# Sums of a Strassen first product made in PSUM instead of by VectorE additions

## The chip, the cores and the metric

The kernel runs on one core of one Trainium2 chip. The metric is the device time in microseconds (us) of one execution; four runs of the kernel before lie between 708.72 and 708.87 us with a median of 708.79. A profile is one such execution, recorded by the hardware.

## The reference, cut to what matters

```python
# x: (8, 8, 512, 64)   state: (8, 8, 32, 64)
a     = softmax(x @ state^T / 8)              # over the 32 states
xread = a @ state                             # 512 tokens a batch
sread = softmax(state @ x^T / 8) @ x          # 32 tokens a batch
t = concat([xread, sread], axis=2) -> (8*544, 512)
h = t @ w_in                                  # 512 -> 2048
g = h * sigmoid(1.702 * h)
out = g @ w_out                               # 2048 -> 512
```

All of it is float32. The loop that matters here is the first product `h` for the 512 `xread` tokens of a batch. The kernel never forms `xread`: per batch it multiplies `state` into `w_in` once (the tiles `M`, 256 rows of head and state by 2048) and then makes `h` as attention weights times `M`, a product over 256 instead of 512.

## The kernel before, in words

All instructions are put in order by the program text (`manual_schedule`): each engine works through its own list in that order, and a semaphore wait that Tile adds stops everything behind it on that engine.

Batches 0 and 1 go through plain products (`up_x`, `down`, lines 524 and 542) while the weights arrive. Batches 2 to 7 and, last, the 256 `sread` tokens ("sr") use Strassen's scheme in Winograd's form, in which a product of 2 x 2 blocks takes seven block products and some sums instead of eight block products.

The first product of such a stage is `up_strassen` (line 1031). It makes `h` in four blocks u = 0..3. A block holds four rooms in SBUF, `c11`, `c12`, `c21`, `c22`: two tiles of 128 rows of `h` from the lower half of the 2048 and two from the upper half, each for the first and the second 256 tokens. Each of the seven block products is four matmul records of 128x128 by 128x256 in the trace (two matmuls, each run as two passes), all recorded at line 1051. Three PSUM banks serve a block: `x` in one of two banks of the pool `psH`, `y` and `z` in two of the four fixed banks `bank_o`. TensorE gathers in a bank only what lies in one chain of matmuls. Where the scheme adds a product to two places, VectorE does it. In the code of before, with `P1` for `l11*b11`:

- `begin(u)` makes `P1` in `x`, ScalarE copies it to `c21` (line 1074); `y = m2*t2`; VectorE writes `c12 = y + c21`.
- `middle(u)` makes `z = m1*t1`; `x += l12*b21`, and gelu of it goes to `c11`; `y += l21*t3`; VectorE writes `c22 = y + c21` and then `c22 = z + c22`; gelu in place.
- `end(u)` makes `y += l22*t4`, VectorE writes `c21 = y + c21`, gelu in place; `z += m4*b22`, VectorE writes `c12 = z + c12`, gelu in place. It is called one block later, after `begin(u + 1)`.

That is five additions of 128x512 on VectorE a block (line 1061, the helper `add`), one copy (line 1074) and four gelus (line 1058) on ScalarE. `s12` (lines 565 and 566) and `s3` (line 571) are the sums of finished rooms that the second product wants: `s12(u - 1)` stands at the end of `end(u)`, and all four `s3` in `rest`. `rest` also holds `end(3)`; it is called from a hook inside the second product's first block product, `P1` of `strassen_two` (line 738), after half of it. `between` puts two sums of the left operands on VectorE after block 0 and two after block 1. The `sr` stage has half as many tokens and no `between`, but ten VectorE steps in `beside`, of which `aside` takes one at three places in each block.

The second product, `strassen_two`, is again Winograd's scheme, five of whose block products are split once more (`strassen_low`, matmuls at line 689); the softmax of the next batch is hung into it by hooks. Its last low product ends just before `up_strassen` of the next batch; it leaves two reads of `psH` banks by VectorE (line 694) behind.

Of the kernel before, what the change touches and what calls it, by code (L numbers as in the profile page):

```python
# [10 lines left out]
FP32 = mybir.dt.float32  # L11
# [3 lines left out]
ALU = mybir.AluOpType  # L15
# [5 lines left out]
def kernel(  # L21
# [30 lines left out]
    nc = tc.nc  # L52
# [5 lines left out]
    P = 128  # L58
# [5 lines left out]
    FC = 512  # L64
# [22 lines left out]
    psH = ctx.enter_context(tc.tile_pool(name="psH", bufs=2, space=bass.MemoryType.PSUM))  # L87
# [4 lines left out]
    def att_ps(shape, name):  # L92
        return psA.tile(shape, FP32, tag="att", name=name)
# [26 lines left out]
    bank_o = [psO.tile([P, FC], FP32, tag=f"o{i}", name=f"o_{i}") for i in range(4)]  # L120
# [72 lines left out]
    for i, v in enumerate((8.0 * most, 8.0 * (most - least))):  # L193
        t = konst.tile([P, 1], FP32, name=f"edge_{i}")
# [360 lines left out]
    def quarters(key, u, ntok):  # L555

        g, half = G[key, u], ntok // 2
        return g[:, :, :half], g[:, :, half:ntok]

    def s12(key, u, ntok):  # L560

        half = ntok // 2
        (a11, a21), (_, a22) = quarters(key, u, ntok), quarters(key, HF // 2 + u, ntok)
        s1, s2 = S1[:, 2 * u : 2 * u + 2, :half], S2[:, 2 * u : 2 * u + 2, :half]
        nc.vector.tensor_tensor(out=s1, in0=a21, in1=a22, op=ALU.add)
        nc.vector.tensor_tensor(out=s2, in0=s1, in1=a11, op=ALU.subtract)

    def s3(key, u, ntok):

        a11, a21 = quarters(key, u, ntok)  # L570
        nc.vector.tensor_tensor(out=a21, in0=a11, in1=a21, op=ALU.subtract)
# [58 lines left out]
    NU, QT = HF // 2, S // 2  # L630
# [400 lines left out]
    def up_strassen(b, ntok, left, right, between=(), beside=()):  # L1031


        beside = list(beside)
        QT = ntok // 2
        b11, b21, b22, t1, t2, t3, t4 = right
        banks = {}

        def product(u, bank, lhs, rhs, first):
            if first:  # L1040
                if bank == "x":
                    banks[bank, u] = psH.tile([P, 2, QT], FP32, tag="h", name=f"upx_{b}_{u}")
                else:
                    o = bank_o[2 * (u % 2) + (bank == "z")]
                    banks[bank, u] = o[:, : 2 * QT].rearrange("p (k t) -> p k t", k=2)
            ps = banks[bank, u]
            n = len(lhs)
            for k in range(2):
                o = 2 * P * (u % 2) + P * k
                for i in range(n):  # L1050
                    nc.tensor.matmul(  # L1051
                        ps[:, k], lhs[i][:, o : o + P], rhs[i],
                        start=(first and k == 0 and i == 0), stop=(i == n - 1), skip_group_check=True,
                    )
            return ps

        def gelu(dst, src):
            nc.scalar.activation(out=dst, in_=src, func=AF.Gelu_apprx_sigmoid)  # L1058

        def add(ps, x, dst):  # L1060
            nc.vector.tensor_tensor(out=dst, in0=ps, in1=x, op=ALU.add)  # L1061

        def aside():
            if beside:
                fn, args = beside.pop(0)
                fn(*args)


        def begin(u):
            l11, l12, l21, l22, m1, m2, m4 = left(u)  # L1070
            G[b, u], G[b, NU + u] = free.pop(0), free.pop(0)
            _, c12 = quarters(b, u, ntok)
            c21, _ = quarters(b, NU + u, ntok)
            nc.scalar.copy(c21, product(u, "x", l11, b11, True))
            add(product(u, "y", m2, t2, True), c21, c12)
            aside()

        def middle(u):
            l11, l12, l21, l22, m1, m2, m4 = left(u)
            c11, c12 = quarters(b, u, ntok)  # L1080
            c21, c22 = quarters(b, NU + u, ntok)
            z = product(u, "z", m1, t1, True)
            gelu(c11, product(u, "x", l12, b21, False))
            add(product(u, "y", l21, t3, False), c21, c22)
            add(z, c22, c22)
            gelu(c22, c22)
            aside()

        def end(u):
            l11, l12, l21, l22, m1, m2, m4 = left(u)  # L1090
            c11, c12 = quarters(b, u, ntok)
            c21, c22 = quarters(b, NU + u, ntok)
            add(product(u, "y", l22, t4, False), c21, c21)
            gelu(c21, c21)
            add(product(u, "z", m4, b22, False), c12, c12)
            gelu(c12, c12)
            aside()
            if u:
                s12(b, u - 1, ntok)

        for u in range(NU):
            begin(u)
            if u:
                end(u - 1)
            middle(u)
            for fn, args in between[u] if u in between else ():
                fn(*args)

        def rest():
            end(NU - 1)  # L1110
            s12(b, NU - 1, ntok)
            for u in range(NU):
                s3(b, u, ntok)

        return rest

# [151 lines left out]
    for b in range(1, B):  # L1268
        if b > 1:
            ahead = {"P1a": [(up_strassen(b, S, *parts_x(b), A[b]["sums"]), ())]}  # L1270
        else:
            ahead = {
                "P1a": [(low_third, (B22,)), (T_of, (T4, B21, T2)), (low_third, (T2,)), (low_away, (4, T4)), (low_third, (T4,))]
            }
# [4 lines left out]
        else:  # L1279

            steps, left, right = sr_sums()
# [12 lines left out]
        k = 3 if b + 1 < B else 0  # L1294
# [6 lines left out]
    strassen(  # L1301
        "sr", B * Ns, lambda r, n: out_s[nb * r.start : nb * r.stop, :, n],
        [[(up_strassen("sr", B * Ns, left, right, beside=beside), ())]],
    )

# [29 lines left out]
```

## Time and profile before

| | |
|---|---|
| median of the runs | 708.79 us |
| the profiled execution | 708.87 us, of which the span in the trace is 707.1 us |
| a batch's stage, from one `up_strassen` to the next | 75.63 us (280.22 less 204.59) |
| of it, from the first matmul of `up_strassen` to the first at line 738 | 22.45 us |
| share of the span, PE / DVE / ACT | 98% / 85% / 33% |
| `add` at line 1061 | 140 instructions, 88.0 us |
| gelus at line 1058 | 84 from SBUF, 49.8 us; 24 + 4 from PSUM |
| copy at line 1074 | 24 of 128x512, median 0.571 us; 4 of 128x256, 0.354 us |

PE is TensorE's matmuls and PEld its loads of the stationary operand, which run beside the matmul ahead; DVE is VectorE, ACT ScalarE. A matmul's length in the trace is longer than the time to the next one, since matmuls are pipelined; here the time between starts counts.

### The profile page before, as it was taken

The page shows a single profiled execution, that of the slowest core. Times are in us where ns is not written, and L with a number is a line of the kernel's source. Part 1 is how long each engine was busy: PE and PEld are TensorE (multiplying, and loading weights), DVE is VectorE, ACT ScalarE, POOL GpSimd, SP SyncE. Part 2 cuts the span into 40 slices and gives each one's busy share as a digit, 9 for nine tenths or more (in the row PEclk, how much of TensorE's full clock was granted, in tenths as well). Part 3 has the DMA queues.
Part 4 walks back from the last instruction along what each step waited for, and adds up shares of the span by engine and source line. Part 5 has one row for each costly group of instructions (what it writes and reads, how often), then busy time and mean ns, then how long its engine had stood idle before and what let it go on. Part 6 is the DMA issues. An engine that isn't in the chain of part 4 may idle for free.

```text
span 707.1 us, 12669 instructions
## 1 busy us (share of the span) xinstructions
PE 694.3 (98%) x4975; PEld 557.3 (79%) x4975; DVE 602.2 (85%) x1246; ACT 230.8 (33%) x456; POOL 0.8 (0%) x8
## 2 busy tenths in 40 slices
PE   7989999999999999999999999999999999999996
PEld 3433544458998799879988899889987998899995
DVE  6999799999978998799978996899789987888650
ACT  5686520013224413433243423341243124200210
POOL 0000000000000000000000000000000000000000
PEclk9999999999999999999999999999999999999999
DMA  8921346228842384409550765048432840041001
GB/s 233 362 77 52 92 152 148 117 89 197 222 116 38 61 194 144 71 7 192 162 106 1 153 180 120 17 82 198 135 52 48 194 149 16 0 125 56 16 1 29
DMA packets 143914, 77.89 MB, mean 110 GB/s; under 512 B 113904, under 2 KB 127728, under 8 KB 143856
## 3 DMA queue, kind: packets, MB, share of 16 engines
q1 hardware_dynamic: 143856, 77.09, 42.3%
q8 instruction: 39, 0.64, 0.4%
q14 instruction: 19, 0.16, 0.1%
HBM read 61.08 MB, written 15.99 MB: 109 GB/s over the span
## 4 chain that ended last, share of the span: by engine, by line
PE 95%; ACT 2%; DMA 2%; SPq 0%; DVE 0%; issue 0%; DVEq 0%
PE low L689 21%; PE o L1051 17%; PE o L738 14%; PE o L689 10%; PE o L542 8%; PE h L524 7%; PE upx L1051 6%; PE M L320 4%; PE o L585 2%; PE o L320 1%; PE warm L125 1%; PE sr L500 1%; PE upx_sr L1051 1%; DMA out_dram<-osb_sr 1%; DMA xn<-in_x_dram 1%; ACT low L219 1%
## 5 line engine op out<-in xcount | busy, mean ns | idle before, releaser
L1061 DVE TENSOR_TENSOR g<-o,g 128x512 f32<-128x512 f32 (+1 forms) x140 | 88.0, 650 | 51.1 <-PE o L1051 50.2
L738 PE MATMUL o<-w_out,g 128*128 128x256 f32 x448 | 100.5, 380 | 0.0
L738 PEld LDWEIGHTS o<-w_out,g 128*128 128x128 f32 x448 | 84.2, 190 | 16.9 <-issue 5.5
L1058 ACT ACTIVATE g<-g 128x512 f32<-128x512 f32 (+1 forms) x84 | 49.8, 600 | 100.8 <-DVE g L1061 100.8
L1051 PE MATMUL upx<-aT,M 128*128 128x256 f32 x192 | 49.3, 379 | 0.0
L1051 PE MATMUL o<-ta,M 128*128 128x256 f32 x192 | 49.3, 379 | 0.0
L1051 PE MATMUL o<-ta,ms 128*128 128x256 f32 x192 | 48.3, 379 | 0.0
L689 PE MATMUL low<-low,g 128*128 128x128 f32 x336 | 44.4, 275 | 0.0
L689 PEld LDWEIGHTS low<-low,g 128*128 128x128 f32 x336 | 40.9, 192 | 0.0
L1051 PEld LDWEIGHTS o<-ta,ms 128*128 128x128 f32 x192 | 36.5, 190 | 5.0
L1051 PEld LDWEIGHTS o<-ta,M 128*128 128x128 f32 x192 | 36.5, 190 | 5.0
L460 ACT COPY M<-M 128x512 f32<-128x512 f32 x64 | 33.1, 598 | 22.2 <-PE M L320 22.2
L1051 PEld LDWEIGHTS upx<-aT,M 128*128 128x128 f32 x192 | 36.0, 190 | 4.6
L689 PE MATMUL low<-sums,later 128*128 128x128 f32 x280 | 37.1, 275 | 0.0
L689 PEld LDWEIGHTS low<-sums,later 128*128 128x128 f32 x280 | 34.6, 192 | 0.4
L320 PE MATMUL M<-w_in,stT 64*32 64x512 f32 x512 | 32.0, 594 | 0.0
L527 ACT ACTIVATE g<-h 128x512 f32<-128x512 f32 x24 | 14.0, 591 | 54.7 <-PE h L524 54.7
L524 PE MATMUL h<-low,M 128*128 128x512 f32 x64 | 29.5, 597 | 1.4 <-DVE low L408 1.4
L524 PE MATMUL h<-aT,M 128*128 128x512 f32 x64 | 28.7, 599 | 1.4 <-ACT M L460 1.4
L689 PE MATMUL low<-w_out,g 128*128 128x128 f32 x224 | 29.6, 275 | 0.0
L542 PE MATMUL o<-w_out,g 128*128 128x512 f32 x64 | 28.6, 594 | 0.0
L542 PE MATMUL o<-w_out,sums 128*128 128x512 f32 x64 | 28.3, 592 | 0.0
(210 smaller groups left out, 1293.4 us busy)
## 6 DMA issues: line engine op xcount, KB each, us to landing
low<-low SPq DMA_DIRECT2D x78, 256.0 KB, 3.7
later<-in_moe_w_out_dram SPq DMA_DIRECT2D x16, 512.0 KB, 3.5
xn<-in_x_dram SPq DMA_DIRECT2D x28, 256.0 KB, 4.8
low<-low SPq DMA_DIRECT2D x9, 768.0 KB, 4.0
w_out<-in_moe_w_in_dram SPq DMA_DIRECT2D x12, 512.0 KB
xsq<-in_x_dram SPq DMA_DIRECT2D x96, 64.0 KB, 2.5
out_dram<-osb SPq DMA_DIRECT2D x18, 256.0 KB, 2.6
out_dram<-later SPq DMA_DIRECT2D x14, 256.0 KB, 2.2
```

The lines of the kernel that those rows point to most:

```text
L125: nc.tensor.matmul(ps, zeros[:, :P], zeros, start=True, stop=True)
L320: nc.tensor.matmul(ps[g][st], A[b]["stT"][rows, st], rhs(rows, j), start=True, stop=True)
L460: nc.scalar.copy(m[:, g], ps[g])
L524: nc.tensor.matmul(hps, lhs[i], rhs[i], start=(i == 0), stop=(i == n - 1))
L527: nc.scalar.activation(out=G[key, f // 2][:, f % 2, :ntok], in_=hps, func=AF.Gelu_apprx_sigmoid)
L542: nc.tensor.matmul(ops, G[key, f // 2][:, f % 2, P * r : P * (r + 1)], w_out[:, f], start=(f == 0), stop=(f == NF - 1))
L585: nc.tensor.matmul(ps[:, r], lhs[f][:, P * r : P * (r + 1)], rhs[:, f], start=(first and r == 0 and f == 0), stop=(f == HF - 1), skip_grou ...
L689: nc.tensor.matmul(ps, lhs[f], rhs[:, f], start=(first and f == 0), stop=(f == QF - 1), skip_group_check=True)
L738: nc.tensor.matmul(ps[:, r], lhs[f][:, P * r : P * (r + 1)], rhs[:, f], start=(r == 0 and f == 0), stop=(f == HF - 1), skip_group_check=True,)
L1051: nc.tensor.matmul(ps[:, k], lhs[i][:, o : o + P], rhs[i], start=(first and k == 0 and i == 0), stop=(i == n - 1), skip_group_check=True,)
L1058: nc.scalar.activation(out=dst, in_=src, func=AF.Gelu_apprx_sigmoid)
L1061: nc.vector.tensor_tensor(out=dst, in0=ps, in1=x, op=ALU.add)
```

## The change

The first block product is now copied by ScalarE from its bank to a second bank of PSUM, and TensorE goes on adding there. A block has four banks: `X` (pool `psH`), `Y` (`bank_o[0]` or `bank_o[3]`), `Z` (`bank_o[2]` or `bank_o[1]`) and `W` (`bank_o[1]` for block 0, else the pool `psA`). `seed(u)` copies `X` to `Y`. `Y += m2*t2` then holds `P1 + m2*t2`; ScalarE copies that to `c12`, and VectorE writes `Z = W + c12`, with `W = m1*t1`. `Y += l21*t3` is copied to `c22`, VectorE adds `W` there, and gelu follows in place. `Y += l22*t4` and `Z += m4*b22` are final: gelu reads both from PSUM.

A block thus has two additions on VectorE, and three copies and four gelus on ScalarE. The order on TensorE changes too: `X` of the next block is made before this block's `Y`, `l22*t4` of block u comes in block u + 1, and `m4*b22` closes its own block. `s12(u - 1)` and `s3(u - 1)` now stand together in block u. `rest` is left with `l22*t4` and the sums of block 3 alone. Matmuls are as many as before.

```diff
-        def begin(u):
-            ...
-            nc.scalar.copy(c21, product(u, "x", l11, b11, True))
-            add(product(u, "y", m2, t2, True), c21, c12)
-            aside()
-        def middle(u):
-            ...
-            z = product(u, "z", m1, t1, True)
-            gelu(c11, product(u, "x", l12, b21, False))
-            add(product(u, "y", l21, t3, False), c21, c22)
-            add(z, c22, c22)
-            gelu(c22, c22)
-            aside()
-        def end(u):
-            ...
-            add(product(u, "y", l22, t4, False), c21, c21)
-            gelu(c21, c21)
-            add(product(u, "z", m4, b22, False), c12, c12)
-            gelu(c12, c12)
-            aside()
-            if u:
-                s12(b, u - 1, ntok)
-        for u in range(NU):
-            begin(u)
-            if u:
-                end(u - 1)
-            middle(u)
-            ...
+        def Y(u):
+            return view(bank_o[3 * (u % 2)])
+        def Z(u):
+            return view(bank_o[2 - u % 2])
...
+        def first_x(u):
+            X[u] = view(psH.tile([P, FC], FP32, tag="h", name=f"upx_{b}_{u}"))
+            product(X[u], u, left(u)[0], b11, True)
+        def first_w(u):
+            W[u] = view(bank_o[1] if u == 0 else att_ps([P, FC], f"upw_{b}_{u}"))
+            product(W[u], u, left(u)[4], t1, True)
+        def seed(u):
+            nc.scalar.copy(Y(u), X[u])
+        def last_y(u):
+            product(Y(u), u, left(u)[3], t4)
+            gelu(quarters(b, NU + u, ntok)[0], Y(u))
+        def sums_after(u):
+            s12(b, u, ntok)
+            s3(b, u, ntok)
+        first_x(0)
+        seed(0)
+        first_w(0)
+        for u in range(NU):
+            ...
+            if u + 1 < NU:
+                first_x(u + 1)
+            product(Y(u), u, m2, t2)
+            nc.scalar.copy(c12, Y(u))
+            add(Z(u), W[u], c12)
+            aside()
+            if u:
+                last_y(u - 1)
+            if u + 1 < NU:
+                seed(u + 1)
+            product(X[u], u, l12, b21)
+            gelu(c11, X[u])
+            if u:
+                sums_after(u - 1)
+            product(Y(u), u, l21, t3)
+            nc.scalar.copy(c22, Y(u))
+            add(c22, W[u], c22)
+            gelu(c22, c22)
+            aside()
+            if u + 1 < NU:
+                first_w(u + 1)
+            product(Z(u), u, m4, b22)
+            gelu(c12, Z(u))
+            ...
+            aside()
         def rest():
-            end(NU - 1)
-            s12(b, NU - 1, ntok)
-            for u in range(NU):
-                s3(b, u, ntok)
+            last_y(NU - 1)
+            sums_after(NU - 1)
```

More of the change, by code (lines that the diff above doesn't have):

```diff
@@ L1036, in up_strassen, with view, product @@
         b11, b21, b22, t1, t2, t3, t4 = right
[L1037 to L1046, printed above, removed]
+        X, W = {}, {}
+        def view(t):
+            return t[:, : 2 * QT].rearrange("p (k t) -> p k t", k=2)
+        def Y(u):
+            return view(bank_o[3 * (u % 2)])
+        def Z(u):
+            return view(bank_o[2 - u % 2])
+        def product(ps, u, lhs, rhs, first=False):
             n = len(lhs)
@@ L1054, in product, with add @@
                     )
-            return ps
         def gelu(dst, src):
             nc.scalar.activation(out=dst, in_=src, func=AF.Gelu_apprx_sigmoid)
-        def add(ps, x, dst):
-            nc.vector.tensor_tensor(out=dst, in0=ps, in1=x, op=ALU.add)
+        def add(out, ps, x):
+            nc.vector.tensor_tensor(out=out, in0=ps, in1=x, op=ALU.add)
         def aside():
@@ L1070, in begin @@
+        def sums_after(u):
[5 more added lines that the diff above has]
+        for u in range(NU):
             l11, l12, l21, l22, m1, m2, m4 = left(u)
             G[b, u], G[b, NU + u] = free.pop(0), free.pop(0)
-            _, c12 = quarters(b, u, ntok)
-            c21, _ = quarters(b, NU + u, ntok)
-            nc.scalar.copy(c21, product(u, "x", l11, b11, True))
-            add(product(u, "y", m2, t2, True), c21, c12)
@@ L1076, in begin @@
-            aside()
-        def middle(u):
-            l11, l12, l21, l22, m1, m2, m4 = left(u)
             c11, c12 = quarters(b, u, ntok)
             c21, c22 = quarters(b, NU + u, ntok)
-            z = product(u, "z", m1, t1, True)
-            gelu(c11, product(u, "x", l12, b21, False))
-            add(product(u, "y", l21, t3, False), c21, c22)
-            add(z, c22, c22)
+            if u + 1 < NU:
+                first_x(u + 1)
+            product(Y(u), u, m2, t2)
+            nc.scalar.copy(c12, Y(u))
@@ L1086, in middle @@
+            add(Z(u), W[u], c12)
[11 more added lines that the diff above has]
+            add(c22, W[u], c22)
             gelu(c22, c22)
             aside()
-        def end(u):
-            l11, l12, l21, l22, m1, m2, m4 = left(u)
-            c11, c12 = quarters(b, u, ntok)
-            c21, c22 = quarters(b, NU + u, ntok)
-            add(product(u, "y", l22, t4, False), c21, c21)
-            gelu(c21, c21)
-            add(product(u, "z", m4, b22, False), c12, c12)
-            gelu(c12, c12)
-            aside()
-            if u:
-                s12(b, u - 1, ntok)
```

## The prediction

> **What bounds the kernel now.** I read the page's busy shares first, then the chain that ended last, then one `up_strassen` stage in the timeline, engine by engine.
>
> The page (busy time and share of each engine, then the chain by engine):
>
> ```profile
> PE 694.3 (98%) x4975; PEld 557.3 (79%) x4975; DVE 602.2 (85%) x1246; ACT 230.8 (33%) x456; POOL 0.8 (0%) x8
> ...
> PE 95%; ACT 2%; DMA 2%; SPq 0%; DVE 0%; issue 0%; DVEq 0%
> ```
>
> The chain is TensorE for 95%, and VectorE, which the change relieves, has 0% of it. A share is an average, so I look at the stage: the busy times by stretch (columns: stretch, length, PE, PEld, DVE, ACT, POOL, clock, DMA share, GB/s). The first row is batch 3's `up_strassen` up to the first matmul of line 738, the second the second product that precedes it, the third the `sr` stage.
>
> ```profile
> 280.22:302.66 22.44, 22.44 (x106) 19.76 (x105) 16.43 (x26) 11.23 (x18) 0.00 (x0) 1.00 0.34 65
> ...
> 652.09:675.31 23.22, 23.22 (x210) 23.22 (x209) 15.00 (x32) 6.43 (x17) 0.00 (x0) 1.00 0.04 14
> 227.04:280.22 53.18, 53.18 (x500) 47.55 (x499) 49.97 (x114) 13.97 (x33) 0.00 (x0) 1.00 0.52 129
> ```
>
> TensorE is busy in every one of the 22.44 us, at clock 1.00. Busy can hide a short stall, so count: 26 block products lie in it, and their starts stand 0.863 us apart:
>
> ```profile
> 280.22 1.03 PE L1051 MATMUL upx<-aT,M 128*128 128x256 f32 x4
> 281.08 1.89 PE L1051 MATMUL o<-ta,ms 128*128 128x256 f32 x8
> 282.81 1.03 PE L1051 MATMUL upx<-aT,M 128*128 128x256 f32 x4
> 283.67 1.03 PE L1051 MATMUL o<-ta,M 128*128 128x256 f32 x4
> ```
>
> 26 x 0.863 = 22.44. There is no stall in this stage to win back. VectorE is busy for 16.43 us of it, and outside, at 49.97 of 53.18 us, it keeps TensorE waiting hardly at all. So the change can win only what little VectorE costs elsewhere, and can lose wherever its new order makes TensorE wait.
>
> **The change, part by part.**
>
> VectorE. Three additions a block go, in 24 blocks of 512 tokens and 4 of `sr`: 72 x 0.690 + 12 x 0.417 = 54.7 us of busy time. The sums of line 571 move from `rest` into the blocks; with two additions and two sums of line 565/566 also gone from there, VectorE enters the second product some seven instructions of about 0.62 us, 4.3 us, earlier. All this lies beside TensorE, hidden today and after. What it can return shows in the low products, where two neighbours of six records each differ:
>
> ```profile
> 331.30 0.83 PE L689 MATMUL o<-sums,later 128*128 128x128 f32 x6
> 331.97 0.88 PE L689 MATMUL low<-sums,g 128*128 128x128 f32 x6
> ```
>
> Six records take 0.83 us in the one and 0.88 in the other, in a bank that VectorE has only just read: a stall of 0.05 us. The starts of all matmuls show two such places a batch (here and at 338.27, 0.07 us) that neither a change of shape nor a DMA explains. Bounds: nothing, and 0.12 x 6 = 0.7 us. I take 0.2, nearer the lower end, because a read that follows its product at once does not come earlier when VectorE has less to do.
>
> ScalarE. Two copies a block are added. The nearest row is the copy of the same shape out of a PSUM bank, and for gelu both sources have a row (counts, then shortest/median/longest in ns, first and last start):
>
> ```profile
> L1074 ACT COPY g<-upx x24: 567/571/585, 205.7 to 601.3; 128x512 f32<-128x512 f32 x24
> ```
>
> ```profile
> L1058 ACT ACTIVATE g<-g x84: 416/630/632, 210.6 to 681.2; 128x512 f32<-128x512 f32 x72, 128x256 f32<-128x256 f32 x12
> L1058 ACT ACTIVATE g<-upx x24: 597/597/597, 208.2 to 604.5; 128x512 f32<-128x512 f32 x24
> L1058 ACT ACT_TABLE_LOAD x6: 1283/1283/1283, 206.3 to 584.4; - x6
> ```
>
> A stage gains 8 x 0.571 = 4.6 us and saves 8 x 0.033 where gelu reads PSUM: 11.23 becomes some 15.5 of 22.44 us. ScalarE is no bound in the mean. A copy from PSUM to PSUM (`seed`) has no row: bounds 0.265 us (the 128x128 copy of line 698, which no 128x512 one can beat) and twice the 0.571; I take 0.571, whose read side and shape are the same.
>
> TensorE. As many matmuls as before, so its busy time is unchanged; only waits count. I walk the new order with the durations above, with T = 0 at the first matmul of `X(0)`. From the rows: products 0.863 apart; a reader starts 1.06 after its product's first matmul (281.28 against 280.22); the load of a product's first stationary operand, which carries the wait, starts 0.21 ahead of its matmul (280.87 against 281.08); and it starts 0.06 after ScalarE's end (in batch 0, 13.23 against 12.10 + 1.07).
>
> ```profile
> 280.87 1.70 PEld L1051 LDWEIGHTS o<-ta,ms 128*128 128x128 f32 x8
> ```
>
> ```profile
> 12.10 1.07 ACT L311 COPY xT<-xT 128x512 f32<-128x512 f32 x2 [1.34 <-PE xT L310]
> 13.23 0.62 PEld L320 LDWEIGHTS o<-xT,stT 64*32 64x32 f32 x32 [0.96 <-ACT xT L311]
> ```
>
> ScalarE at the head of batch 3's stage:
>
> ```profile
> 281.28 0.58 ACT L1074 COPY g<-upx 128x512 f32<-128x512 f32 x1 [4.17 <-PE upx L1051]
> 281.88 1.28 ACT L1058 ACT_TABLE_LOAD   x1
> 283.87 0.60 ACT L1058 ACTIVATE g<-upx 128x512 f32<-128x512 f32 x1 [0.70 <-PE upx L1051]
> ```
>
> Block 0 on TensorE: `X(0)` 0, `W(0)` 0.86, `X(1)` 1.73, `Y += m2*t2` 2.59, `X += l12*b21` 3.45, `Y += l21*t3` 4.32, `W(1)` 5.18, `Z` 6.04, then `X(2)` 6.91.
>
> - `seed(0)` 1.06 to 1.64; `Y` at 2.59 has 0.7 us in hand.
> - The copy of `Y` to `c12` runs 3.65 to 4.23, and `Y += l21*t3` may not overwrite `Y` before it ends. The load could start at 4.29; it is due at 4.11. **A new wait of 0.15 to 0.18 us**, since in block 0 one product only, not two, stands between the two uses of `Y`. Before, VectorE's read of `y` had `z` and `x` (two products) ahead of the next use.
> - Behind the copy: `seed(1)` to 4.8, the table load to 6.1, gelu of `X(0)` to 6.7. `X(2)` wants that bank; its load is due at 6.70 + 0.17. In hand: 0.1 us, so about nothing.
> - VectorE's `Z = W + c12` runs 4.3 to 5.0, due 5.8: hidden by `W(1)` and its wait.
>
> In blocks 1 to 3, `l22*t4` of the block before stands between, and the same walk (c12 copy, `c21` gelu, seed, `c11` gelu, c22 copy, wait for VectorE, `c22` gelu, `c12` gelu) leaves 0.4 us at the tightest place, `Y += l21*t3` of block 1, and 0.7 or more later. `c22`'s gelu now waits on ScalarE's own list with the `c12` gelu and the next block's copy queued behind it, until VectorE has done the three sums and the addition; that is in those margins. The second product's first matmuls find their rooms ready 1.5 us early. In block 2 a load waits for both VectorE and ScalarE, which costs one more sequencer instruction: nothing to 0.07 us.
>
> `sr`: products 0.893 apart, copies 0.354 and gelus 0.383 long; the tight place has 0.1 us in hand. Nothing. The DMA tail behind the last products keeps its place.
>
> Sum: 6 x 0.17 = 1.0 us more, 0.2 less, on the profiled execution's 708.87 us: 709.7. That execution stands 0.08 above the median: **709.6 us**. As 0.2% (1.42 us) is about what a measurement of this kernel tells from no change, this counts as the same.
>
> **The rule that speaks against it.** The row: the copy ends at 281.86, the table load starts at 281.88 and takes 1.28, and at line 372 the exp behind such a load starts 0.01 us after its end:
>
> ```profile
> 319.07 1.28 ACT L372 ACT_TABLE_LOAD   x1
> 320.36 0.69 ACT L372 ACTIVATE e<-o,mx 128x512 f32<-128x512 f32 x1
> ```
>
> So a switch costs 1.3 us, and the walk uses that. The Trainium skill, page "ScalarE: Activation LUTs", section "What ACT_TABLE_LOAD costs", puts a drain of about 1.38 us on top, 2.66 in all. By that the gelu of `X(0)` would end 1.4 us later and `X(2)` wait some 1.2 us a batch: 709.6 + 7 = 717 us. The traced loads show no such drain. On `seed`, the same page ("Step-by-step: what each stage is for") says that ScalarE writes to PSUM sooner than to SBUF; no row here shows it, and by it the sum would stay 709.6, as a shorter seed alters no wait above.
>
> **The rivals.**
>
> 1. All hidden: the copy ends 0.17 us sooner than I walk it, or the load can wait without delaying its matmul. 708.79 - 0.2 = 708.6 us. For it: the load takes 0.19 of the 0.216 us between matmuls, so a little is free. Against it: only 0.03 is.
> 2. Slower, by `seed` in block 0. ScalarE's list runs `seed(1)`, table load, gelu of `X(0)` without a gap, and that gelu releases the bank of `X(2)`. Each 0.1 us by which `seed`, or a copy that VectorE's PSUM traffic slows, exceeds 0.57 goes to TensorE once the 0.1 in hand is used: it decides from a seed of about 0.67. At 1.14 it is 0.45 us a batch more, and 6 x (0.17 + 0.45) = 3.7: 712.3 us. For it: ScalarE then reads and writes PSUM at once, as nothing in this trace does. Against it: ScalarE's copies out of PSUM run at the same 0.57 to 0.60 everywhere, whatever VectorE does.
> 3. Faster, VectorE being what paces TensorE: then part of the 54.7 us would come back, 700 us or less. Against it: TensorE starts 26 products in 26 spacings, and VectorE is idle 6 of 22.44 us. The bound of what can come back is the 0.7 us above, 708.1 us.
>
> **How the numbers follow.** Forecast (a wait of 0.05 to 0.25 us a batch) 0.58, all hidden 0.17, seed 0.20, VectorE 0.05. The forecast's upper end, with the extra sequencer instruction (6 x 0.32 = 1.9 us), crosses 0.2%: about a sixth of it, 0.10. Slower: 0.20 + 0.10 = 0.30; faster 0.04; same 0.66. The range goes from 708.2 (rival 3's bound) to 712.0 (nearly rival 2's full price).
>
> **What would show it.** Right: line 1061's successor with 56 additions; in each of six stages a gap of about 0.17 us ahead of the sixth product, ended by ScalarE's copy; stages of about 75.8 us. Wrong: a seed over 0.67 us, a gap ahead of the ninth product, waits in blocks 1 to 3, or a stage under 75.6 us.

## The result, and the profile after

The changed kernel takes 709.65 us (median of 33 runs, 709.44 to 710.55), the kernel before 708.85 us (median of 53). The ratio is 1.0011 with a 95% interval of 1.0006 to 1.0016: 0.80 us slower.

The page of the changed kernel, busy time and share of each engine, and the chain by engine:

```profile
PE 696.1 (98%) x4975; PEld 557.1 (79%) x4975; DVE 551.4 (78%) x1162; ACT 257.5 (36%) x512; POOL 0.8 (0%) x8
...
PE 95%; ACT 2%; DMA 2%; SPq 0%; DVE 0%; issue 0%; DVEq 0%
```

VectorE lost 84 instructions and 50.8 us, ScalarE gained 56 and 26.7 us. The chain looks as before: TensorE, with nothing of VectorE in it.

Where the 0.80 us are, the stages show. In the profile of before, one `up_strassen` starts 75.63 us after the other; now it is 280.53 - 204.77 = 75.76 us, and five stages in a row have that length to within 0.01 us. From the first matmul of batch 2's stage to the last matmul of the program it is 497.26 us against 496.47. This measure is finer than the run times: the stretch ahead of that first matmul, which the change leaves as it was, took 204.2 to 205.1 us in the profiles of this study, and a spread as large is there at the program's hundredth matmul, some 18 us in.

The waits of TensorE's loads between 204 and 602 us in the changed kernel (us in total, times, longest):

```profile
PEld M L320 <- issue: 6.9, 25, 0.3
PEld o L738 <- issue: 4.2, 5, 0.8
PEld o L689 <- issue: 4.2, 5, 0.8
PEld o L320 <- issue: 1.7, 5, 0.3
PEld o L1054 <- ACT g L1100: 1.6, 6, 0.3
```

The last line is new: six waits, one a stage, for the copy of `Y` to `c12` at line 1100. The others are spacing between matmuls of other shapes. The place in batch 3, on the load side, on the matmul side and on ScalarE:

```profile
283.77 0.84 PEld L1054 LDWEIGHTS upx<-aT,M 128*128 128x128 f32 x4
284.88 0.73 PEld L1054 LDWEIGHTS o<-ta,M 128*128 128x128 f32 x4 [0.27 <-ACT g L1100]
```

```profile
283.12 1.03 PE L1054 MATMUL o<-ta,ms 128*128 128x256 f32 x4
283.99 1.03 PE L1054 MATMUL upx<-aT,M 128*128 128x256 f32 x4
284.88 1.13 PE L1054 MATMUL o<-ta,M 128*128 128x256 f32 x4
285.85 1.03 PE L1054 MATMUL upw<-ta,ms 128*128 128x256 f32 x4
```

```profile
281.60 0.57 ACT L1079 COPY o<-upx 128x512 f32<-128x512 f32 x1 [4.17 <-PE upx L1054]
284.24 0.58 ACT L1100 COPY g<-o 128x512 f32<-128x512 f32 x1 [2.08 <-PE o L1054]
284.72 0.59 ACT L1079 COPY o<-upx 128x512 f32<-128x512 f32 x1
285.33 1.28 ACT L1060 ACT_TABLE_LOAD   x1
286.63 0.60 ACT L1060 ACTIVATE g<-upx 128x512 f32<-128x512 f32 x1
287.12 0.58 ACT L1112 COPY g<-o 128x512 f32<-128x512 f32 x1
```

`Y += m2*t2` starts at 283.12, its copy runs from 284.24 to 284.82, and the load for `Y += l21*t3` starts 0.06 us later. It was due 0.21 us ahead of 283.99 + 0.863 = 284.85, at 284.64, so it is 0.24 us late. The product's starts show what that costs: the sixth is at 284.88 instead of 284.85, and the seventh follows 0.97 us later instead of 0.863. Together that is some 0.13 us, as the stages have it, and in six stages 0.79 us, the 497.26 less 496.47 above: the whole difference.

The copy itself starts 1.12 us behind its product's first matmul, where the copy at line 1074 of before starts 1.06 behind. Each copy at line 1100 has a semaphore instruction ahead of it on ScalarE's sequencer (ACTq):

```profile
L1100 ACTq EVENT_SEMAPHORE  x28: 17/17/17, 208.4 to 673.8; - x28
```

The copies at lines 1079 and 1112 have none. Of those that waited for TensorE alone, the copies at line 1100 start 0.47 us behind the last matmul of their product, the others 0.42. That the semaphore instruction makes this difference is likely, but no run takes it away.

### The profile page after: what moved, and what is told of

Same layout as the page of the kernel before. It is cut to its first block, busy times and chain, and to the rows that moved or that the text cites. A ratio compares the mean times of both kernels' runs of the same rounds, so it can differ in the third digit from the quotient of the medians.

```text
span 708.1 us, 12665 instructions
## 1 busy us (share of the span) xinstructions
PE 696.1 (98%) x4975; PEld 557.1 (79%) x4975; DVE 551.4 (78%) x1162; ACT 257.5 (36%) x512; POOL 0.8 (0%) x8
## 4 chain that ended last, share of the span: by engine, by line
PE 95%; ACT 2%; DMA 2%; SPq 0%; DVE 0%; issue 0%; DVEq 0%
PE low L689 21%; PE o L1054 15%; PE o L738 14%; PE o L689 10%; PE o L542 8%; PE h L524 7%; PE upx L1054 6%; PE M L320 4%; PE o L585 2%; PE upw L1054 2%; PE o L320 1%; PE warm L125 1%; PE sr L500 1%; PE upx_sr L1054 1%; DMA out_dram<-osb_sr 1%; DMA xn<-in_x_dram 1%
## 5 line engine op out<-in xcount | busy, mean ns | idle before, releaser
L1060 ACT ACTIVATE g<-o 128x512 f32<-128x512 f32 (+1 forms) x56 | 31.3, 559 | 26.8 <-PE o L1054 26.8
L527 ACT ACTIVATE g<-h 128x512 f32<-128x512 f32 x24 | 14.0, 592 | 54.7 <-PE h L524 54.7
L1063 DVE TENSOR_TENSOR o<-upw,g 128x512 f32<-128x512 f32 x18 | 12.6, 699 | 24.0 <-ACT g L1100 24.0
L698 ACT COPY pu<-low 128x128 f32<-128x128 f32 x21 | 5.6, 265 | 69.6 <-PE low L689 65.3
L1054 PE MATMUL o<-ta,ms 128*128 128x256 f32 x120 | 30.8, 379 | 0.0
```

What stands on the lines that cost most here:

```text
L527: nc.scalar.activation(out=G[key, f // 2][:, f % 2, :ntok], in_=hps, func=AF.Gelu_apprx_sigmoid)
L1054: nc.tensor.matmul(ps[:, k], lhs[i][:, o : o + P], rhs[i], start=(first and k == 0 and i == 0), stop=(i == n - 1), skip_group_check=True,)
L1063: nc.vector.tensor_tensor(out=out, in0=ps, in1=x, op=ALU.add)
```

## The experiments

All compare with the kernel before on the same chip.

### 1. Another product between the two uses of Y

```diff
             if u:
                 sums_after(u - 1)
+            else:
+                first_w(1)
             product(Y(u), u, l21, t3)
...
-            if u + 1 < NU:
+            if u and u + 1 < NU:
                 first_w(u + 1)
```

> The changed kernel, but in block 0 of each stage the product W(1) = m1*t1 is made ahead of Y += l21*t3 instead of behind it, so that two products, not one, stand between the two uses of Y. Nothing else moves. Theory (the wait of 0.134 us a stage is TensorE waiting for ScalarE's copy of Y to c12 to end): the wait goes, 6 x 0.134 = 0.80 us come back, less some 0.02 us a stage because the gelu of X(0) then ends 0.03 us after the load of X(2) is due: 708.85 to 709.0 us, stage 75.63 us. Rival (the stage is longer because ScalarE as a whole has more work, or because matmuls add to a bank that ScalarE wrote): the time stays at 709.65 us and the wait turns up elsewhere.

Measured: 709.05 us, ratio 1.0003 (0.9994 to 1.0012). This is 0.05 us above the range that the theory gave, and the interval is too wide to tell the theory from the rival, so the stages decide: 75.63 us, and 496.50 us from the first matmul of batch 2's stage to the last one. The same waits view has four lines; the fifth is gone:

```profile
PEld M L320 <- issue: 6.9, 25, 0.3
PEld o L738 <- issue: 4.2, 5, 0.8
PEld o L689 <- issue: 4.2, 5, 0.8
PEld o L320 <- issue: 1.7, 5, 0.3
```

The twelve copies and sixteen gelus of a stage are as they were, matmuls still add to a bank that ScalarE wrote (that TensorE gathers in a bank only what lies in one chain holds for the kernel before alone), and the loss has gone with the place of one product. What the change costs is that wait; beyond it 0.03 us are left of 496.5. Nor does anything come back for the additions that VectorE no longer makes.

### 2. The seed twice

```diff
             if u + 1 < NU:
                 seed(u + 1)
+                if u == 0:
+                    seed(1)
```

> The changed kernel, with seed(1) issued twice in block 0 of each stage (the second copy writes the same values). Theory (ScalarE's list seed, table load, gelu of X(0) holds the bank of X(2), with 0.09 us in hand in the profile of the changed kernel): 0.48 to 0.57 us more on that list cost 0.39 to 0.48 us a stage, 2.3 to 2.9 us in all: 712.0 to 712.6 us, with the new gap ahead of the ninth product, X(2). Rival (ScalarE is idle a third of the stage, so one copy more is hidden): 709.65 us.

Measured: 712.17 us, ratio 1.0048 (1.0035 to 1.0062); stages of 76.17 us, 0.41 more than the changed kernel's. ScalarE, then TensorE, in batch 3:

```profile
284.78 1.19 ACT L1079 COPY o<-upx 128x512 f32<-128x512 f32 x2
285.99 1.28 ACT L1060 ACT_TABLE_LOAD   x1
287.29 0.60 ACT L1060 ACTIVATE g<-upx 128x512 f32<-128x512 f32 x1
```

```profile
286.77 1.03 PE L1054 MATMUL o<-aT,m 128*128 128x256 f32 x4
287.94 1.13 PE L1054 MATMUL upx<-aT,M 128*128 128x256 f32 x4
288.90 1.03 PE L1054 MATMUL o<-ta,ms 128*128 128x256 f32 x4
```

The waits view of this run has one line more than the changed kernel's:

```profile
PEld upx L1054 <- ACT g L1060: 3.3, 6, 0.5
```

The new gap is where the theory has it: `X(2)` comes 1.17 us after `Z` instead of 0.863, as it needs the bank that the gelu of `X(0)`, 287.29 to 287.89, gives back. 0.6 us more on ScalarE's list cost 0.41. ScalarE is idle a third of the stage, and that does not help: the order on its list decides.

### 3. The seed twice, the table load early

```diff
+    gate = konst.tile([P, 1], FP32, name="gate")
...
         first_x(0)
+        gelu(gate, one)
         seed(0)
```

> As the run before, with seed(1) twice, but a gelu of one column is issued ahead of seed(0), so that the table load of 1.28 us falls into the 4 us in which ScalarE is idle before the stage. Theory (the load is on the list ahead of the gelu of X(0), and Y's copy to c12 alone makes the wait ahead of the sixth product): the gap ahead of X(2) goes, the 0.134 us ahead of Y += l21*t3 stay: 709.6 to 709.75 us. Rival (the table load is also what delays the sixth product): 708.85 us. Rival (ScalarE's total is what counts): over 711 us.

Measured: 709.26 us (708.98 to 709.83), ratio 1.0006 (0.9997 to 1.0014). That is 0.34 us under the range that the theory gave, and the interval holds both that range and the first rival's 708.85, so the run time alone proves little. The stages settle it: 75.77 us, the changed kernel's length, and of the two waits of experiment 2 only one is left, untouched:

```profile
PEld o L1055 <- ACT g L1102: 1.6, 6, 0.3
```

(Line 1055 is the matmul, 1102 the copy to `c12`.) The load of 1.28 us now runs while ScalarE has nothing to do; the gap ahead of `X(2)` is gone, the 0.13 us at the sixth product stay, so the table load has no part in them. In the profiled execution the time is missing ahead of batch 2's stage, which starts at 204.16 us here and at 204.77 in the changed kernel's profile. The program's hundredth matmul already starts at 17.14 us here and at 17.84 there, long before the gelu of one column. Why is not settled.

### 4. VectorE's relief alone

```diff
-            add(product(u, "y", l21, t3, False), c21, c22)
-            add(z, c22, c22)
+            product(u, "y", l21, t3, False)
+            add(z, c21, c22)
...
-            add(product(u, "y", l22, t4, False), c21, c21)
-            gelu(c21, c21)
-            add(product(u, "z", m4, b22, False), c12, c12)
-            gelu(c12, c12)
+            gelu(c21, product(u, "y", l22, t4, False))
+            gelu(c12, product(u, "z", m4, b22, False))
```

> The kernel before, with three of the five VectorE additions of a block taken out and nothing put in their place: c22 is made of z + c21 without y, and the gelus of c21 and c12 read the banks y and z directly. Left out are thus the sums that these additions made; matmuls and their order are those of before. It relieves VectorE as the change does, with no new copy on ScalarE. Theory (VectorE does not pace TensorE; the two short stalls of 0.05 and 0.07 us a batch are not its backlog): 708.75 to 708.9 us. The prediction's share of 0.2 us come back: 708.65 us. Rival (VectorE's time is on the path): 700 to 707 us.

Measured: 708.93 us, ratio 1.0000 (0.9991 to 1.0009); stages of 75.63 us. The page, and batch 3's `up_strassen` (columns as in the prediction):

```profile
PE 695.6 (98%) x4975; PEld 557.8 (79%) x4975; DVE 552.9 (78%) x1162; ACT 228.8 (32%) x456; POOL 0.8 (0%) x8
...
280.45:302.90 22.45, 22.45 (x106) 19.77 (x105) 12.42 (x20) 11.21 (x19) 0.00 (x0) 1.00 0.34 65
```

VectorE falls from 85% to 78% of the span, from 16.43 to 12.42 us in this stretch, and not a hundredth of a microsecond a stage comes back. The two short stalls in the low products stand where they stood, at 0.05 and 0.07 us. So neither the 54.7 us of rival 3 nor the 0.2 us that the prediction took for returned are to be had.

### 5 and 6. Another room for one result at the end

The end of the changed kernel's profile shows a wait of another kind. The last two additions on VectorE, and what they waited for:

```profile
698.80 3.62 PE L585 MATMUL o<-w_out,g 128*128 128x256 f32 x16
699.50 0.43 DVE L604 TENSOR_TENSOR osb_sr<-o,g 128x256 f32<-128x256 f32 x1 [3.48 <-DMA out_dram<-osb_sr]
703.36 0.42 DVE L604 TENSOR_TENSOR osb_sr<-o,g 128x256 f32<-128x256 f32 x1 [3.43 <-DMA out_dram<-osb_sr]
```

The results share one buffer, `osb`, and each addition waits for the transfer of the one ahead. The matmuls of the last one start at 698.80, sixteen at 0.216 us, so its bank is ready near 702.5.

```diff
-            o = opool.tile([P, nb, HN], FP32, tag="osb", name=f"osb_{key}_{i}{k}")
+            if (i, k) == (1, 0):
+                o = later[:, 0, : nb * HN].rearrange("p (r n) -> p r n", r=nb)
+            else:
+                o = opool.tile([P, nb, HN], FP32, tag="osb", name=f"osb_{key}_{i}{k}")
```

On the kernel of experiment 1:

> The changed kernel with W(1) made ahead of Y += l21*t3 in block 0, as in the first run of the study, and in the last second product the result of rows 1, columns 0 goes to a room of the tile later (whose operands are spent) instead of the one buffer osb, which then is free for the last result. In the profile of the changed kernel the last addition starts at 703.36 us, held by the DMA out of osb, 0.86 us after its bank was ready. Theory: stages of 75.63 us as before, and 0.85 us less behind them: 0.8 us under the kernel before, 708.1 us. Rival (the last DMA only waits elsewhere, behind the one ahead of it): no gain, as the kernel before.

On the kernel before:

> The kernel before, with the same other room for one result of the last second product. Theory: the gain of 0.85 us at the end has nothing to do with the change: 708.0 us, the same as the run before within 0.1 us. Rival (it needs the changed kernel's idle VectorE): as the kernel before.

Measured: 708.02 us, ratio 0.9989 (0.9980 to 0.9998), and 708.01 us, ratio 0.9987 (0.9979 to 0.9996). The end in experiment 5:

```profile
697.61 3.62 PE L585 MATMUL o<-w_out,g 128*128 128x256 f32 x16
697.82 0.42 DVE L607 TENSOR_TENSOR later<-o,g 128x256 f32<-128x256 f32 x1 [2.97 <-PE o L585]
698.27 0.54 SPq L608 DMA_DIRECT2D out_dram<-later  x1
701.27 0.42 DVE L607 TENSOR_TENSOR osb_sr<-o,g 128x256 f32<-128x256 f32 x1 [3.03 <-PE o L585]
```

The last addition now waits for TensorE, 3.66 us behind the first of its matmuls instead of 4.56. The intervals end just below 1, but both versions end within 0.01 us of each other, 0.8 us ahead of the kernel before: the gain has nothing to do with the change.

### 7. A small step moved behind a release

The stall of 0.05 us that the prediction showed in a low product has a likely cause in the trace: the load there starts 0.05 us behind the end of an addition of VectorE that reads its bank (line 694, `later<-low,pu`), and on VectorE's list `x_inverse` (lines 435 and 436) stands ahead of that addition. In the changed kernel, VectorE and then the load:

```profile
331.59 0.18 DVE L435 TENSOR_SCALAR sm<-sm 128x32 f32<-128x32 f32 x1
331.81 0.35 DVE L436 RECIPROCAL sm<-sm 128x32 f32<-128x32 f32 x1
332.08 0.23 DVE L694 TENSOR_TENSOR later<-low,pu 128x128 f32<-128x128 f32 x1
332.22 0.68 DVE L441 TENSOR_TENSOR e<-e,sm 128x512 f32<-128x512 f32 x1
332.82 0.28 DVE L694 TENSOR_TENSOR later<-o,later 128x128 f32<-128x128 f32 x1
```

```profile
332.36 0.97 PEld L689 LDWEIGHTS low<-sums,g 128*128 128x128 f32 x8
```

```diff
-            ("P6.1", x_sum, 0), ("P6.3", x_sum, 1), ("P6.3", x_inverse), ("P6.4", x_scale, 0),
+            ("P6.1", x_sum, 0), ("P6.3", x_sum, 1), ("P6.4", x_inverse), ("P6.4", x_scale, 0),
```

> As the run with W(1) first and the other room, and the small steps x_inverse (two instructions of 128x32 on VectorE) stand one hook later, P6.4 instead of P6.3, behind the low product's addition instead of ahead of it. Theory (the stall of 0.05 us a batch in a low product is that addition, which releases the bank, standing behind x_inverse on VectorE, and is no backlog): the stall goes in the five batches that have it, stages of 75.58 us, 0.24 us less: 707.85 us. Rival (it is a fixed cost of the change of bank): stages stay at 75.63 us.

Measured: 710.10 us, ratio 1.0017 (1.0008 to 1.0026): 2.1 us slower than experiment 5, not 0.24 faster. Stages are 75.94 us, one of them 76.29. VectorE, TensorE's loads and its matmuls at the same place (the edit shifts line 694 to 697 and 689 to 692):

```profile
331.89 0.29 DVE L697 TENSOR_TENSOR later<-low,pu 128x128 f32<-128x128 f32 x1 [0.17 <-PE low L692]
332.10 0.17 DVE L435 TENSOR_SCALAR sm<-sm 128x32 f32<-128x32 f32 x1
332.30 0.35 DVE L436 RECIPROCAL sm<-sm 128x32 f32<-128x32 f32 x1
332.69 0.69 DVE L441 TENSOR_TENSOR e<-e,sm 128x512 f32<-128x512 f32 x1
333.30 0.28 DVE L697 TENSOR_TENSOR later<-o,later 128x128 f32<-128x128 f32 x1
```

```profile
332.47 0.97 PEld L692 LDWEIGHTS low<-sums,g 128*128 128x128 f32 x8
333.64 0.97 PEld L692 LDWEIGHTS o<-low,later 128*128 128x128 f32 x8 [0.19 <-DVE later L697]
```

```profile
332.58 1.06 PE L692 MATMUL low<-sums,g 128*128 128x128 f32 x8
333.64 1.16 PE L692 MATMUL o<-low,later 128*128 128x128 f32 x8
334.63 0.28 PE L692 MATMUL low<-w_out,g 128*128 128x128 f32 x1
```

The first addition now runs as soon as its product is done, and the 0.05 us there are gone: that much of the theory holds. But `x_inverse` now stands between this addition and the next one, which releases the bank of the product after, where only `x_scale` (line 441) stood before. That addition ends at 333.58, and the load waits for it: the products follow each other 1.06 and 0.99 us apart instead of 0.89, 0.26 us in all. The second stall that the prediction named grows with it, from 0.07 to 0.16 us, and 0.26 + 0.09 - 0.05 = 0.30 us is, to 0.01, what the stage is longer. In the stage of 76.29 us the second stall is 0.51:

```profile
491.38 0.97 PEld L692 LDWEIGHTS o<-w_out,spare_M 128*128 128x128 f32 x8 [0.44 <-DVE later L697]
```

Why VectorE came later in this one stage is not settled. The theory looked at the release ahead of the step and not at the one behind. In this stretch a product takes 0.89 us, and from one of the two additions to the next VectorE's list took 0.74 (332.08 to 332.82 above), so half a microsecond ahead of either of them reaches TensorE. VectorE, which has no part in the chain of the kernel before, delays TensorE here through the order of its list. The second stall was not taken on by itself.

## Why the prediction was right, point by point

709.6 was predicted and 709.65 measured, inside the range, and the small loss comes from the wait that the forecast named. That the sum is right to 0.05 us is luck: two of its terms were too large by some 0.2 us each, one a loss and one a gain, and cancel.

- **What bounds the kernel.** Right. The stage has no stall to win back, and experiments 1 and 4 give 0.00 us a stage for VectorE's relief. Rival 3 is out.
- **The wait at `Y += l21*t3` of block 0.** Right in place and cause (the six waits of the waits view; experiment 1 takes them away), mis-sized: 0.17 taken, 0.13 measured, so 0.80 us for the predicted 1.0. Both halves of the term were off. The copy started 1.12 us behind its product's first matmul, not 1.06, so that the load was 0.24 late, not 0.18; and I charged a late load in full, while the matmul followed its load at once, at 284.88 with it, and 0.11 us of the lateness vanished.
- **The 0.2 us back from VectorE.** Wrong, 0.0 measured. The step that failed is the one from the two stalls to VectorE's amount of work: both stand as they were with three additions a block gone (experiment 4) and in the changed order (experiment 1). The one of 0.05 us is made by a step that stands ahead of one addition in the list (experiment 7), and relief elsewhere does not move it. At the one of 0.07 us the load also starts 0.05 us behind the end of an addition of VectorE (338.18, then 338.23 in the profile of before); what would move that one is open.
- **The seed.** Taken as 0.571 us, measured 0.570 in the median; the one on the list ahead of `X(2)`, `seed(1)` at 284.72, took 0.59, within the 0.1 us in hand. ScalarE's copies out of PSUM do not all run at 0.57 to 0.60, as the prediction has it: some at line 460 take 0.62 right behind another. Rival 2 did not come, and its price was right: a second seed cost 0.41 us a stage and 712.17 us, where the rival said 0.45 and 712.3 for a seed of twice the length.
- **The table load.** The gelu starts at 286.63, 0.02 us behind the end of the load, though ScalarE was busy right up to it. The page "ScalarE: Activation LUTs" of the Trainium skill, section "What ACT_TABLE_LOAD costs", adds a drain of some 1.38 us; this trace has none, and the estimate of 717 us that was worked out from it did not come.
- **The margins.** `X(2)` was given 0.1 us in hand: the gelu ends at 287.23, its load starts at 287.36, 0.06 of that being the usual distance. No wait in blocks 1 to 3 nor in `sr`, as walked; the second sequencer instruction in block 2 cost nothing that shows.

## What to carry to other kernels

Where one engine starts its work without a gap, taking work off another cannot pay, however busy that one is; before moving sums to a third engine, count the starts in the stage. What such a change can cost is read from the order: walk each bank or buffer from its last reader to its next writer and count the products between, above all in the first turn of a loop, where the product that gives the distance later is still missing. And a step moved out of the way of one release stands in the way of the next: both sides of its new place have to be walked.

## What the runs showed of the hardware that was not expected

- A load of the stationary operand that starts 0.24 us late delays its matmuls by 0.13 us only: the first matmul starts together with its load (284.88 us both), the second comes 0.10 us late, and from there on the beat is the regular one. In experiment 2 the load of `X(2)` starts 0.51 us late and costs 0.41, again some 0.1 us less.
- A copy by ScalarE of 128x512 that starts after a pause takes 0.570 us from PSUM to PSUM (line 1079) and 0.585 from PSUM to SBUF (line 1100; line 1074 of before also): 0.015 us less. The page "ScalarE: Activation LUTs" of the Trainium skill, section "Step-by-step: what each stage is for", says that PSUM is the sooner target; for these copies it is, by that little. Right behind another instruction the order is not so: 0.567 to 0.573 us to SBUF (line 1074 of before), 0.570 or 0.593 to PSUM (line 1079).
- A copy of 128x512 starts 0.48 us behind the start of the copy ahead of it (284.24, 284.72), but the table load starts only when the copy ahead has ended (284.72 + 0.59, then 285.33).
